# Spreading the reciprocals of the softmax sums over a tile: two products with the identity instead of a copy and a transpose

## The chip, the cores and the metric

One core of one Trainium2 chip. The metric is the device time of the whole kernel in microseconds (us). The engines: TensorE (PE, matrix products; PEld is its loading of the stationary operand), VectorE (DVE), ScalarE (ACT), GpSimd (POOL), SyncE (SP, which issues DMAs). Each engine executes its own instructions in order and waits for the others by semaphores.

## The reference

Three stages, each feeding the next, all fp32:

```python
# attention: q, k, v of 2 x 8 heads x 576 x 64
scores = q @ k.T / 8
kth = 32nd largest of each row
scores = where(scores >= kth, scores, -1e9)
attn = exp(scores - max); attn = attn / (sum(attn) + 1e-9)
x = (attn @ v), heads side by side          # 1152 x 512
# experts: 4 of 512 -> 1024 -> 512, weighted by the token's probabilities
x = sum over e of p[:, e] * (relu(x @ w1[e]) @ w2[e])
# last stage: 512 -> 768 three times, maximum, back to 512
out = max(x @ w1, x @ w2, x @ w3) @ w_out
```

## The kernel before

The 1152 tokens are nine tiles of 128, the 16 heads eight pairs of heads, four to a batch. A unit of the attention is one token tile of one head pair: 36 of them, called pairs here too, numbered `n` from 0. A pair computes the scores of both heads (`pss`, L475 or L483), finds the 32 largest of each row on VectorE (L513, L515), makes masked exponentials `p` with their row sums `rs` on ScalarE, turns `p` around with transposes on TensorE (`psp`, L559 and L564, copied to `pt` by ScalarE at L562 and L567), and multiplies with v.

The steps that the change touches come at the end of a pair. `guard` (L572, ACT) adds 1e-9 to the two sums of each token, and `recip` (L578, DVE) makes `rr`, 128 tokens x 2 heads, the reciprocals. The product with v stands transposed, `psv`, 128 features (64 of each head) x 128 tokens, so the reciprocals are needed as a tile of the same shape, the one of head j for token t in all rows j*64 to j*64+63 of column t. `spread` (L582, ACT) copies `rr` with a broadcast to `rb`, 128 tokens x 2 x 64. `trans_r` (L587, PE) transposes it to `psr`, and ACT copies that to `r` (L589). `norm` (L611, DVE) multiplies `psv` by `r`, which gives `xt`, and `split_x` (L624, ACT; L625, POOL) takes it apart into a high and a low half, `xh` and `xl`, for the expert stage's products.

`pv` (L591 to L606) is one product of 128 stationary columns (L601) and eight of 64 (L604): for each of four key tiles one for head 0, written to partitions 0 to 63 of `psv`, and one for head 1, written to partitions 64 to 127. An fp32 matmul shows as two records in the trace, a transpose as one.

The expert stage keeps its own products in flight beside the attention. A product of it is three matmuls of halves (L764, L765, L766); the halves of weights come from ACT (`whi`, L269) and from POOL or DVE (`wlo`, L275), the halves of the hidden layer from ACT and DVE, or, for every fourth hidden tile, from ACT (L902, L903) and POOL (L904). The first token tile uses whole fp32 weights (L850, L865).

The order is written by hand. A pair has eight slots, and tables of options (L39 to L45: FIRST, MIDDLE, TIGHT and so on, picked by `n`) say at which slot after `8 * n` a step stands; `at_slot` puts one step there, and `two` puts one there and its second half (the copy out of the bank) `lag` slots later. `rec` is the slot of the reciprocal, `pv` that of the product with v. Between slots the main loop places the expert stage's steps so that PE's budget of columns (`pe(...)`) keeps up with VectorE's (`dve(...)`). After the slots end, at about 446 us, the rest of the experts and the last stage run alone.

Of the kernel before, what the change touches and what calls it, by code (L numbers as in the profile page):

```python
# [10 lines left out]
F32 = mybir.dt.float32  # L11
# [3 lines left out]
AF = mybir.ActivationFunctionType  # L15
# [22 lines left out]

FIRST = dict(stag=2, new=1, scores=-12, trans=11, pv=17, rec=16, lag=2, sum=4, late=1)  # L39
MIDDLE = dict(stag=2, new=1, scores=-12, at=(11, 12), pv=14, rec=12, lag=1, sum=0, late=1)  # L40
TIGHT = dict(stag=3, new=1, scores=-7, at=(10, 11), guard=11, rec=11, spread=12, pv=12, turn=12, norm=13, split=13, last=14, lag=0, lag_s=1, sum=0, late=1)
SECOND = dict(TIGHT, norm=14, split=14, last=15)
THIRD = dict(stag=4, new=1, scores=-4, at=(11, 12), guard=12, rec=13, spread=13, pv=14, turn=14, norm=15, split=15, last=16, lag=0, lag_s=2, sum=0)
BOTH = dict(stag=4, new=1, scores=-4, at=(14, 14), pv=17, rec=15, lag=2, lag_t=1, sum=0, late=1)
LOOSE = dict(stag=4, new=1, scores=-4, at=(14, 14), pv=17, rec=15, split=22, last=24, lag=2, sum=0)  # L45

# [15 lines left out]
def kernel(  # L62
# [14 lines left out]
    nc = tc.nc  # L77
    B, HP, D, _, S = k.shape
    NT, DM = out.shape
    E = gates.shape[2]  # L80
    P = 128
# [13 lines left out]
    def batches(t):  # L95
        return (0, 1) if t == MIXED else (0 if t < MIXED else 1,)
# [16 lines left out]
    at = ctx.enter_context(tc.tile_pool(name="at", bufs=2))  # L113
# [7 lines left out]
    ident = const.tile([P, P], F32, name="ident")  # L121
# [12 lines left out]
    def pe(n):  # L134
        clock["pe"] += n / 2400.0

    def bank(name):
        return pg.tile([P, 512], F32, tag="g", name=name)
# [306 lines left out]
    class Pair:  # L445
# [131 lines left out]
            dve(60)  # L577
            nc.vector.reciprocal(out=self.rr, in_=self.rs)  # L578

        def spread(self):  # L580
            self.rb = at.tile([P, 2, D], F32, tag="rb", bufs=1, name="rb")
            nc.scalar.activation(out=self.rb, in_=self.rr.unsqueeze(2).to_broadcast([P, 2, D]), func=AF.Copy)  # L582

        def trans_r(self):
            ps = bank("psr")
            pe(260)
            nc.tensor.transpose(ps[:, 0:P], self.rb.rearrange("p a d -> p (a d)"), ident)  # L587
            self.r = at.tile([P, P], F32, tag="r", name="r")
            return lambda: [nc.scalar.activation(out=self.r, in_=ps[:, 0:P], func=AF.Copy), self.did.add("r")]  # L589

# [36 lines left out]
    def attention():  # L627

        NP = len(pairs)
        prs = {}  # L630
        later, between = {}, {}

        def options(n):
            return TIGHT if n == HP - 1 else SECOND if n == 2 * HP - 1 else MIDDLE if n in (HP - 2, 2 * HP - 3, 2 * HP - 2) else FIRST if n < 2 * HP else THIRD if n == 3 * HP - 1 else BOTH if n in ON_ACT[1] else LOOSE

        def at_slot(s, f, *a):
            later.setdefault(s, []).append((f, a))


        first_use = {}  # L640
        for n, (c, hp, t) in enumerate(pairs):
            for b in batches(t):
                if ("v", b, hp) not in first_use:
                    first_use["v", b, hp] = n
                    at_slot(8 * n + (options(n)["pv"] - 7 if b and hp else 0), load_v, b, hp)
                if t >= FULL:
                    first_use.setdefault(("k", b, hp), n)
            if t >= FULL and (t, hp) not in later_scores:
                first_use.setdefault(("q", c, hp), n)
            elif n and t < FULL:  # L650
                o = options(max(0, n - 2))
                at_slot(max(8 * n + options(n)["scores"] - LOAD_FULL, 8 * (n - 2) + o["scores"] + o["stag"] + 1), load_full, n)
        free = {"k": -99, "q": -99}
        for key, n in first_use.items():
            if key[0] == "v":
                continue
            s0 = 8 * n
            load, split = (load_k, split_k) if key[0] == "k" else (load_q, split_q)
            at = max(s0 + options(n)["scores"] - (SPLIT_K if key[0] == "k" else SPLIT_Q), free[key[0]] + 2)
            if key[0] == "k" and key[1] and key[2]:  # L660

                at = max(at, 8 * pairs.index((MIXED, key[2] - 1, MIXED)) + options(n)["scores"] + options(n)["stag"] + (1 if key[2] == HP - 1 else 4))
            at_slot(max(at - LOAD, free[key[0]] + 1), load, *key[1:])
            at_slot(at, split, *key[1:])
            free[key[0]] = at
        for n, (c, hp, t) in enumerate(pairs):
            s0 = 8 * n
            prs[n] = Pair(n)
            pr = prs[n]
            o = options(n)  # L670

            def two(s, f, *a, lag=o["lag"]):
                at_slot(s, lambda: at_slot(s + lag, f(*a)))
            for j in range(2):
                b0 = s0 + o["stag"] * j
                two(b0 + o["scores"] - SOONER * ((t, hp) in later_scores), pr.scores, j, lag=o.get("lag_s", o["lag"]))
                for i in range(7):
                    if o["new"]:
                        later.setdefault(b0 + i, []).insert(0, (pr.topk, (j, i)))
                    else:  # L680
                        at_slot(b0 + i, pr.topk, j, i)
                at_slot(b0 + 2, pr.negate, j)
                at_slot(b0 + 5, pr.exp, j)
                late = o.get("late", MASK_LATE) * pr.on_act[j]
                two(b0 + 7 + late, pr.mask, j, lag=o["sum"] if n < EARLY else 3)
                two(s0 + o["at"][j] if "at" in o else b0 + o["trans"] + late + (late > 0), pr.trans_p, j, lag=o.get("lag_t", o["lag"]))
            two(s0 + o["at"][1] if "at" in o else s0 + o["stag"] + o["trans"], pr.trans_p, 2, lag=o.get("lag_t", o["lag"]))
            at_slot(s0 + o.get("guard", o["rec"] - 1), pr.guard)
            at_slot(s0 + o["rec"], pr.recip)
            if o is LOOSE:  # L690
                at_slot(s0 + o["rec"], at_slot, s0 + o["rec"] + 1, pr.spread)
            else:
                at_slot(s0 + o.get("spread", o["rec"] + 1), pr.spread)
            at_slot(s0 + o["pv"], pr.pv)
            two(s0 + o.get("turn", o["rec"] + 2), pr.trans_r)
            end = max(o["pv"], o["rec"] + 2) + o["lag"]
            if n == 1:
                at_slot(s0, nc.sync.dma_start, gate, gates)
            if n == HP - 1:
                between.setdefault(s0 + o["norm"], []).append((norm_gates, ()))  # L700
            if "norm" in o:
                between.setdefault(s0 + o["norm"], []).append((pr.norm, ()))
            else:
                at_slot(s0 + end + 1, pr.norm)
            two(s0 + o.get("split", end + 2), pr.split_x)
        at_slot(-5, load_soon)
        two(9, two_soon, 0, lag=1)
        two(13, two_soon, 1, lag=3)
        for i, t in enumerate((7, *SOON_TWO, 6)):
            at_slot(17 + 3 * i, store_soon, t)  # L710
        last = {}
        for n, p in enumerate(pairs):
            o = options(n)
            last[p[0:2]] = 8 * n + o.get("last", max(o["pv"], o["rec"] + 2) + 2 * o["lag"] + 2)
        for n in range(len(alone)):
            at_slot(ALONE_FROM + ALONE_STEP * n, load_alone, n + 1)
        end = max(last.values()) + 1
        s = min(later)
        while s <= end:
            todo = later.pop(s, [])  # L720
            i = 0
            while i < len(todo):
                f, a = todo[i]
                f(*a)
                todo[i + 1:i + 1] = between.pop(s, [])
                todo += later.pop(s, [])
                i += 1
            if s > 8 * NP + 2:
                clock["dve"] += PAUSE
            yield s, [c for c in last if last[c] + (READY if c[1] == HP - 2 else 0) == s]  # L730
            s += 1

        while narrowed[0] < WIDE * len(wide):
            clock["dve"] += PAUSE
            yield s, []
            s += 1


    lag = []
# [31 lines left out]
    def begun(ps, wt, xs, N, parts):  # L771

        for f in range(2):
            for a in parts:

                product(spread(ps[:, f * N:(f + 1) * N], xs[0][a]), [w[:, a, f * P:(f + 1) * P] for w in wt], [x[a] for x in xs], f == a == 0, False)
            yield True
# [397 lines left out]
```

## Time and profile before

| | us |
|---|---|
| median of 3 runs | 735.45 (735.43 to 735.67) |
| the profiled execution, its own time | 734.86 |
| its span, first to last instruction | 733.0 |
| PE busy in the span | 715.2 (98%) |
| DVE, ACT, POOL busy | 580.2, 504.8, 476.7 |
| mean granted clock of TensorE | 1.00 |

The profiled execution is one run of the kernel under the hardware profiler; its span and the 1.86 us around it make its own time. Times of rows are from that one execution. The busy time of an engine is the union of its instructions. A PE record's duration includes its way through the array, so records overlap, and what one costs the next is read from start to start. An entry in square brackets says how long the engine stood still ahead of a row, and whose result ended that.

### The profile page before, as it was taken

How to read it: one execution, taken by the hardware profiler on the slowest of the kernel's cores; microseconds unless marked ns; L12 is line 12 of the kernel's file. 1: busy time of each engine (PE TensorE's matmuls, PEld its weight loads, DVE VectorE, ACT ScalarE, POOL GpSimd, SP SyncE). 2: the span in 40 equal slices, each digit the busy share in tenths (PEclk: the TensorE clock that was granted, in tenths of full speed). 3: DMA queues.
4: the chain of work that ended last, by engine and by line, in shares of the span. 5: the costliest groups of instructions: out<-in, count | busy, mean ns of one | idle time of the engine just before them, and what ended most of it. 6: DMA issues, size and time to landing. Idle time of an engine off the chain costs nothing. (4 is left out here: it accounts for less than half of the span.)

```text
span 733.0 us, 13786 instructions
## 1 busy us (share of the span) xinstructions
PE 715.2 (98%) x4758; PEld 637.1 (87%) x4758; DVE 580.2 (79%) x1174; ACT 504.8 (69%) x1127; POOL 476.7 (65%) x416
## 2 busy tenths in 40 slices
PE   5899999999999999999999999999999999999997
PEld 3687679889999998899988998999889998998996
DVE  7999989989999999999999974766879873323441
ACT  4868889899987886788888876556566753442431
POOL 2514779678989975879779867856745773532520
PEclk9999999999999999999999999999999999999999
DMA  8995555635756553555455436786879855543501
GB/s 238 303 281 203 146 180 156 181 113 165 208 154 197 150 164 111 170 170 177 137 165 173 139 122 216 267 299 209 294 238 338 256 189 211 167 147 114 188 1 43
DMA packets 57813, 135.26 MB, mean 185 GB/s; under 512 B 9936, under 2 KB 23120, under 8 KB 57744
## 3 DMA queue, kind: packets, MB, share of 16 engines
q1 hardware_dynamic: 49248, 125.74, 54.7%
q10 hardware_dynamic: 8496, 8.65, 3.4%
q8 instruction: 37, 0.61, 0.3%
q14 instruction: 32, 0.26, 0.1%
HBM read 123.36 MB, written 11.01 MB: 183 GB/s over the span
## 5 line engine op out<-in xcount | busy, mean ns | idle before, releaser
L275 POOL TENSOR_TENSOR wlo<-raw,whi 128x512 fp32r<-128x512 f32 x252 | 332.0, 1347 | 135.1 <-ACT whi L269 124.8
L269 ACT ACTIVATE whi<-raw 128x1024 fp32r<-128x1024 f32 x164 | 169.9, 1058 | 18.6 <-PE ps L766 10.2
L764 PE MATMUL ps<-xl,whi 128*128 128x256 f32 (+1 forms) x584 | 173.6, 297 | 0.5 <-POOL xl L625 0.5
L766 PE MATMUL ps<-xh,wlo 128*128 128x256 f32 (+1 forms) x584 | 170.7, 292 | 0.0
L765 PE MATMUL ps<-xh,whi 128*128 128x256 f32 (+1 forms) x584 | 170.6, 292 | 0.0
L513 DVE MAX8 m<-work 128x8 f32<-128x576 f32 x216 | 155.1, 744 | 0.1
L764 PEld LDWEIGHTS ps<-xl,whi 128*128 128x128 f32 x584 | 110.8, 190 | 1.6 <-POOL xl L625 0.7
L765 PEld LDWEIGHTS ps<-xh,whi 128*128 128x128 f32 x584 | 109.7, 188 | 0.9 <-issue 0.2
L766 PEld LDWEIGHTS ps<-xh,wlo 128*128 128x128 f32 x584 | 109.7, 188 | 0.0
L515 DVE MATCH_REPLACE8 work<-m,work 128x576 f32<-128x576 f32 x144 | 106.6, 741 | 0.0
L275 DVE TENSOR_TENSOR wlo<-raw,whi 128x1024 fp32r<-128x1024 f32 x38 | 54.7, 1445 | 49.7 <-ACT whi L269 36.8
L764 PE MATMUL ps<-wlo,h 128*128 128x512 f32 x224 | 91.0, 406 | 2.1 <-POOL wlo L275 1.9
L766 PE MATMUL ps<-whi,h 128*128 128x512 f32 x224 | 87.8, 392 | 0.0
L765 PE MATMUL ps<-whi,h 128*128 128x512 f32 x224 | 87.6, 391 | 0.0
L245 POOL TENSOR_TENSOR narrow<-narrow,raw 128x256 int32<-128x256 int32 x48 | 46.5, 976 | 21.3 <-DMA narrow<-narrow 5.7
L513 DVE MAX8 m<-s 128x8 f32<-128x576 f32 x71 | 53.1, 747 | 2.5 <-ACT s L495 2.5
L495 ACT ACTIVATE s<-pss 128x288 f32<-128x288 f32 x128 | 45.5, 401 | 12.0 <-PE pss L475 7.1
L515 DVE MATCH_REPLACE8 work<-m,s 128x576 f32<-128x576 f32 x72 | 53.3, 741 | 0.0
L764 PEld LDWEIGHTS ps<-wlo,h 128*128 128x128 f32 x224 | 42.8, 191 | 11.3 <-POOL wlo L275 5.0
L562 ACT ACTIVATE pt<-psp 128x512 f32<-128x512 f32 x72 | 40.0, 600 | 15.7 <-PE psp L559 15.6
L766 PEld LDWEIGHTS ps<-whi,h 128*128 128x128 f32 x224 | 42.1, 188 | 9.9 <-POOL h L904 0.5
L1042 DVE TENSOR_TENSOR tm<-ps,tm 128x384 f32<-128x384 f32 x36 | 19.8, 556 | 39.0 <-PE ps L766 39.0
(118 smaller groups left out, 1493.7 us busy)
## 6 DMA issues: line engine op xcount, KB each, us to landing
raw<-in_w_dram SPq DMA_DIRECT2D x128, 512.0 KB, 4.3
raw<-narrow SPq DMA_DIRECT2D x36, 512.0 KB, 4.5
raw<-in_m_dram SPq DMA_DIRECT2D x36, 256.0 KB, 5.1
whole<-in_w_dram SPq DMA_DIRECT2D x14, 512.0 KB, 5.5
narrow<-narrow ACTq DMA_DIRECT2D x48, 128.0 KB, 5.0
kraw<-in_k_dram SPq DMA_DIRECT2D x16, 288.0 KB, 4.5
raw<-in_mo_dram SPq DMA_DIRECT2D x12, 256.0 KB, 5.8
kfull<-in_k_dram SPq DMA_DIRECT2D x9, 288.0 KB, 5.2
```

What stands on the lines that cost most here:

```text
L245: nc.gpsimd.tensor_tensor(out=out.bitcast(I32), in0=out.bitcast(I32), in1=last, op=ALU.add)
L269: nc.scalar.activation(out=hi, in_=raw, func=AF.Copy)
L275: on.tensor_tensor(out=lo[:, x], in0=raw[:, x], in1=hi[:, x].bitcast(F32), op=ALU.subtract)
L495: nc.scalar.activation(out=s[:, h, :], in_=halves[h][:, 0:SH], func=AF.Copy)
L513: nc.vector.max(m[:, 8 * r:8 * r + 8], src)
L515: nc.vector.match_replace(out=self.w[j], in_to_replace=m[:, 8 * r:8 * r + 8], in_values=src, imm_value=NEG)
L562: return lambda: [nc.scalar.activation(out=d, in_=ps.rearrange("p (r n) -> p r n", r=NR), func=AF.Copy), self.did.add(("pt", part))]
L764: nc.tensor.matmul(ps, lhsT=lh, rhs=rl, start=first, stop=False)
L765: nc.tensor.matmul(ps, lhsT=lh, rhs=rh, start=False, stop=False)
L766: nc.tensor.matmul(ps, lhsT=ll, rhs=rh, start=False, stop=last)
L1042: nc.vector.tensor_tensor(out=tm[:, g], in0=ps, in1=tm[:, g], op=ALU.max)
```

## The change

The copy `spread` goes, with its places in the option tables. `trans_r` becomes two matmuls into the same bank: for each head j the stationary operand is column j of `rr`, read 64 times with stride zero, and the moving operand is the identity; the result, 64 partitions x 128 tokens, goes to partitions j*64 to j*64+63 of `psr`. `trans_r` now stands at the slot of `pv`. The copy to `r` and all that follows stay. The budget entry of `trans_r`, `pe(260)`, stays.

```diff
--- before.py
+++ after.py
@@ -38,9 +38,9 @@
 
 FIRST = dict(stag=2, new=1, scores=-12, trans=11, pv=17, rec=16, lag=2, sum=4, late=1)
 MIDDLE = dict(stag=2, new=1, scores=-12, at=(11, 12), pv=14, rec=12, lag=1, sum=0, late=1)
-TIGHT = dict(stag=3, new=1, scores=-7, at=(10, 11), guard=11, rec=11, spread=12, pv=12, turn=12, norm=13, split=13, last=14, lag=0, lag_s=1, sum=0, late=1)
+TIGHT = dict(stag=3, new=1, scores=-7, at=(10, 11), guard=11, rec=11, pv=12, norm=13, split=13, last=14, lag=0, lag_s=1, sum=0, late=1)
 SECOND = dict(TIGHT, norm=14, split=14, last=15)
-THIRD = dict(stag=4, new=1, scores=-4, at=(11, 12), guard=12, rec=13, spread=13, pv=14, turn=14, norm=15, split=15, last=16, lag=0, lag_s=2, sum=0)
+THIRD = dict(stag=4, new=1, scores=-4, at=(11, 12), guard=12, rec=13, pv=14, norm=15, split=15, last=16, lag=0, lag_s=2, sum=0)
 BOTH = dict(stag=4, new=1, scores=-4, at=(14, 14), pv=17, rec=15, lag=2, lag_t=1, sum=0, late=1)
 LOOSE = dict(stag=4, new=1, scores=-4, at=(14, 14), pv=17, rec=15, split=22, last=24, lag=2, sum=0)
 
@@ -577,14 +577,11 @@
             dve(60)
             nc.vector.reciprocal(out=self.rr, in_=self.rs)
 
-        def spread(self):
-            self.rb = at.tile([P, 2, D], F32, tag="rb", bufs=1, name="rb")
-            nc.scalar.activation(out=self.rb, in_=self.rr.unsqueeze(2).to_broadcast([P, 2, D]), func=AF.Copy)
-
         def trans_r(self):
             ps = bank("psr")
             pe(260)
-            nc.tensor.transpose(ps[:, 0:P], self.rb.rearrange("p a d -> p (a d)"), ident)
+            for j in range(2):
+                nc.tensor.matmul(ps[j * D:(j + 1) * D, 0:P], lhsT=self.rr[:, j:j + 1].to_broadcast([P, D]), rhs=ident, start=True, stop=True)
             self.r = at.tile([P, P], F32, tag="r", name="r")
             return lambda: [nc.scalar.activation(out=self.r, in_=ps[:, 0:P], func=AF.Copy), self.did.add("r")]
 
@@ -687,12 +684,8 @@
             two(s0 + o["at"][1] if "at" in o else s0 + o["stag"] + o["trans"], pr.trans_p, 2, lag=o.get("lag_t", o["lag"]))
             at_slot(s0 + o.get("guard", o["rec"] - 1), pr.guard)
             at_slot(s0 + o["rec"], pr.recip)
-            if o is LOOSE:
-                at_slot(s0 + o["rec"], at_slot, s0 + o["rec"] + 1, pr.spread)
-            else:
-                at_slot(s0 + o.get("spread", o["rec"] + 1), pr.spread)
             at_slot(s0 + o["pv"], pr.pv)
-            two(s0 + o.get("turn", o["rec"] + 2), pr.trans_r)
+            two(s0 + o["pv"], pr.trans_r)
             end = max(o["pv"], o["rec"] + 2) + o["lag"]
             if n == 1:
                 at_slot(s0, nc.sync.dma_start, gate, gates)
```

VectorE, GpSimd and SyncE keep their orders. TensorE's changes in place only in pairs 0 and 4. Here is TensorE around the product with v in pair 4, before (`psp` are the transposes of the next pair's exponentials, `pss` scores, `hfull` and `whole` the first tile's expert products):

```order
L564 MATMUL psp<-ident,p 128x128
L865 MATMUL ps_783<-whole,hfull 128x512 x4
L601 MATMUL psv<-pt_807,v_last_112 128x128
L604 MATMUL psv<-pt,vt 64x128 x8
L475 MATMUL pss<-kfull,qfull 128x288 x2
L587 MATMUL psr<-ident,rb 128x128
L559 MATMUL psp<-ident,p 128x128 x4
L865 MATMUL ps_783<-whole,hfull 128x512
```

and the same place after the change, where lines have smaller numbers:

```order
L564 MATMUL psp<-ident,p 128x128
L858 MATMUL ps_779<-whole,hfull 128x512 x4
L598 MATMUL psv<-pt_803,v_last_112 128x128
L601 MATMUL psv<-pt,vt 64x128 x8
L584 MATMUL psr<-ident,rr 64x128 x2
L475 MATMUL pss<-kfull,qfull 128x288 x2
L559 MATMUL psp<-ident,p 128x128 x4
L858 MATMUL ps_779<-whole,hfull 128x512
```

The two products for `psr` stand ahead of the two score products, where the transpose stood behind them. In the other pairs but 0 the place is the same. TensorE in pair 22, whose transpose starts at about 284 us, before:

```order
L766 MATMUL ps_3978<-xh,wlo 128x256
L601 MATMUL psv<-pt_3958,v_last_113 128x128
L604 MATMUL psv<-pt,vt 64x128 x8
L587 MATMUL psr<-ident,rb 128x128
L764 MATMUL ps_4045<-xl,whi 128x256
L765 MATMUL ps_4045<-xh,whi 128x256
```

and after:

```order
L759 MATMUL ps_3954<-xh,wlo 128x256
L598 MATMUL psv<-pt_3936,v_last_113 128x128
L601 MATMUL psv<-pt,vt 64x128 x8
L584 MATMUL psr<-ident,rr 64x128 x2
L757 MATMUL ps_4022<-xl,whi 128x256
L758 MATMUL ps_4022<-xh,whi 128x256
```

Two products of 64 stationary columns stand in the place of one transpose. ScalarE in the same pair, before (`rs` are the sums, `raw` and `h` the hidden tile that POOL takes, `whi` a weight's high half):

```order
L572 ACTIVATE rs<-rs 128x2
L520 ACTIVATE nb<-m_3929 128x1
L562 ACTIVATE pt<-psp 128x512 x2
L567 ACTIVATE pt_3958<-psp 128x128
L582 ACTIVATE rb<-rr 128x128
L902 ACTIVATE raw<-ps_3767 128x512
L903 ACTIVATE h<-raw 128x512
L269 ACTIVATE whi<-raw 128x1024 x2
```

and after:

```order
L572 ACTIVATE rs<-rs 128x2
L520 ACTIVATE nb<-m_3907 128x1
L562 ACTIVATE pt<-psp 128x512 x2
L567 ACTIVATE pt_3936<-psp 128x128
L895 ACTIVATE raw<-ps_3746 128x512
L896 ACTIVATE h<-raw 128x512
L269 ACTIVATE whi<-raw 128x1024 x2
```

The copy to `rb` is gone, and the reading of the hidden tile's bank follows the last copy to `pt`.

## Rows read from the trace of the kernel before

**Rows 1.** The page's first part: busy us (share of span) and instructions, by engine.

```profile
PE 715.2 (98%) x4758; PEld 637.1 (87%) x4758; DVE 580.2 (79%) x1174; ACT 504.8 (69%) x1127; POOL 476.7 (65%) x416
```

**Rows 2.** Windows: stretch, its us; busy PE, PEld, DVE, ACT, POOL; clock, DMA, GB/s.

```profile
30.00:60.00 30.00, 29.60 (x231) 24.64 (x232) 29.86 (x71) 23.26 (x70) 5.04 (x7) 1.00 0.95 285
60.00:160.00 100.00, 96.93 (x668) 78.53 (x667) 92.17 (x201) 88.71 (x221) 72.47 (x67) 1.00 0.50 151
160.00:446.00 286.00, 285.11 (x2202) 257.59 (x2201) 270.87 (x576) 232.42 (x543) 237.29 (x204) 1.00 0.54 163
```

**Rows 3.** Groups by line (busy us, mean ns | idle before); L587 in 160:446 (min/median/max).

```profile
L587 PE MATMUL psr<-ident,rb 128*128 128x128 f32 x36 | 11.8, 328 | 0.1
L582 ACT ACTIVATE rb<-rr 128x128 f32<-128x128 f32 x36 | 11.5, 318 | 7.4 <-DVE rr L578 7.3
L587 PE MATMUL psr<-ident,rb x24: 327/328/330, 164.4 to 444.8; 128*128 128x128 f32 x24
```

**Rows 4.** Timeline of PE, 443.7 to 445.5 us: start, us, instruction; second row: last pair.

```profile
443.75 1.09 PE L604 MATMUL psv<-pt,vt 128*64 128x128 f32 x16
444.57 0.28 PE L604 MATMUL psv<-pt,vt 128*64 128x128 f32 x2
444.78 0.33 PE L587 MATMUL psr<-ident,rb 128*128 128x128 f32 x1
444.86 0.48 PE L764 MATMUL ps<-wlo,h 128*128 128x512 f32 x1
445.18 0.39 PE L765 MATMUL ps<-whi,h 128*128 128x512 f32 x1
445.41 0.40 PE L766 MATMUL ps<-whi,h 128*128 128x512 f32 x1
```

**Rows 5.** Timeline of PE, eight transposes of exponentials.

```profile
439.70 1.04 PE L559 MATMUL psp<-ident,p 128*128 128x128 f32 x8
```

**Rows 6.** Timeline of PE behind score products in 64-row tiles, 73.8 us.

```profile
73.80 0.70 PE L865 MATMUL ps<-whole,hfull 128*128 128x512 f32 x1
...
74.33 0.59 PE L865 MATMUL ps<-whole,hfull 128*128 128x512 f32 x1
```

**Rows 7.** Timeline of ACT, 280.7 to 283.5 us.

```profile
280.75 0.29 ACT L567 ACTIVATE pt<-psp 128x128 f32<-128x128 f32 x1
282.68 0.31 ACT L582 ACTIVATE rb<-rr 128x128 f32<-128x128 f32 x1 [1.64 <-DVE rr L578]
282.89 0.58 ACT L902 ACTIVATE raw<-ps 128x512 f32<-128x512 f32 x1
```

**Rows 8.** Timeline of POOL, 284 to 291 us.

```profile
284.21 1.30 POOL L904 TENSOR_TENSOR h<-raw,h 128x512 fp32r<-128x512 f32 x1 [4.26 <-ACT h L903]
285.47 5.58 POOL L275 TENSOR_TENSOR wlo<-raw,whi 128x512 fp32r<-128x512 f32 x4
```

**Rows 9.** Timeline of PE, 289 to 291.6 us; three products between these two.

```profile
288.98 0.40 PE L766 MATMUL ps<-whi,h 128*128 128x512 f32 x1
...
291.10 0.50 PE L764 MATMUL ps<-wlo,h 128*128 128x512 f32 x1 [0.78 <-POOL wlo L275]
```

**Rows 10.** Waits of weight loads, 160:446 (us in total, times, longest).

```profile
PEld psp L564 <- ACT s L495: 0.6, 2, 0.3
PEld psv L601 <- ACT pt L567: 0.5, 2, 0.3
```

**Rows 11.** Waits of PE, 60:160.

```profile
PE ps L764 <- POOL wlo L275: 1.1, 4, 0.3
PE psv L601 <- ACT pt L567: 1.0, 2, 0.7
```

**Rows 12.** Timeline of DVE around pair 11's reciprocal.

```profile
144.52 0.15 DVE L578 RECIPROCAL rr<-rs 128x2 f32<-128x2 f32 x1
144.59 1.40 DVE L513 MAX8 m<-work 128x8 f32<-128x576 f32 x2
```

**Rows 13.** Timeline of PE, pair 11's transpose.

```profile
145.45 0.33 PE L587 MATMUL psr<-ident,rb 128*128 128x128 f32 x1
```

## The prediction

> **What bounds the kernel now.** First the page's line of busy times: TensorE (PE) is busy for 715 of the 733.0 us of the span [rows 1]. Then the windows by stage: what an edit is worth depends on whether PE or something that feeds it is late there. In 30 to 60 us VectorE (DVE) is busy for 29.86 of 30 us, in 60 to 160 us no engine is full (PE idle for 3.07 of 100 us, DVE at 92%, ScalarE (ACT) at 89%), and in 160 to 446 us PE is busy for 285.1 of 286 us [rows 2]. The granted clock of TensorE is 1.00 (its 2.4 GHz level) in each of them, so no term here is one of the clock. Third, the groups by line and shape: where the edited instructions lie. There are 36 transposes at L587 and 36 copies at L582 that feed them; 24 of the transposes start between 164.4 and 444.8 us, in the stretch in which PE decides, and none later [rows 3]. Last, PE's timeline around one transpose, because a matmul's duration (328 ns) is not what it holds PE for: starts count.
>
> **PE, per pair.** Removed: one transpose. Added: two products of 64 stationary columns each, written to the two halves of the partitions. That is the shape of the eight products at L604 that stand directly ahead, and it is the way the order shows them in 34 of 36 pairs. Around 444.8 us the sixteen records of L604 (two for each fp32 product) start within 443.75 to 444.57 in eight pairs, seven steps in .82 us or .12 each; the two of a pair run together [rows 4]. Eight transposes at L559 take 1.04 us, of which the last lasts some .28 like the last pair of L604: (1.04 - .28)/7 = .109 from one to the next [rows 5]. I take .109 for a pair of small records too, the first of L604's steps being longer by what precedes it. The transpose at L587 starts .21 after the last pair, the next product .08 after the transpose, and the one after that .32 later, where such products follow each other by .23 [rows 4]. So the transpose costs about .08 + .09 = .17 us; the .20 ahead of it is the way from 64-column to 128-column tiles and is paid by whatever comes next. After the change: four records in two pairs, 2 x .109 = .218, then the .20, then the next product. One thing comes on top: the first 128-wide product after small tiles takes about .11 longer than its like (.70 against .59 us, L865 at 73.80 and 74.33 [rows 6]). I take +.10. Sum: .218 + .10 - .17 = **+.15 us per pair**. The bounds: if nothing is exposed behind the small tiles, .218 - .17 = +.05; if the two halves do not run together, 4 x .109 - .17 + .10 = +.37. I take the value between, because L604, directly ahead and of the same tiles, pairs up. The stationary operand of stride zero has no row of its own; I cost its load as that of L604's.
>
> In 160 to 446 us this is 24 x .15 = **+3.6 us** on the engine that decides. Nothing covers it: PE is idle there for .9 us in all.
>
> **ACT.** Removed: 36 copies of 318 ns, 11.5 us, and the 7.4 us for which ACT stood still ahead of them, nearly all for the reciprocal of DVE [rows 3]. ACT executes in order, so whatever is queued behind such a copy waits with it. At 282.68 us this can be followed to PE: ACT is through at 281.04, waits 1.64 us for the reciprocal, copies, and only then reads L902's bank (.21 after the copy's start) [rows 7]. From there L903 gives POOL the tile for which it has waited 4.26 us, POOL makes one h and four wlo until 291.05 [rows 8], and PE, which goes through four steps between 288.98 and 291.10 that take .23 each elsewhere, needs 2.12 us for .92: a stall of 1.2 us, plus .1 in the longer first product behind it [rows 9]. Without the copy this chain may begin up to 1.85 us sooner (1.64 + .21), more than the 1.3 us of the stall: **-1.3 us**. What is late next there is PE itself. Weight loads that waited in this stretch for other results of ACT, psp for s (.6) and psv for pt (.5), are 1.1 us in four places [rows 10]; most of these wait for chains that begin at a PE event and have no such copy in them. I take **-0.2**, a fifth; the bounds are 0 and -1.1.
>
> **Before 160 us.** Twelve pairs. Up to 60 us DVE is full [rows 2], its order and work do not change, and PE's extra time lies beside it. In 60 to 160 us PE waits for wlo (1.1 us) and for pt (1.0 us) [rows 11]: chains of POOL and ACT set the pace, and PE's extra .15 falls into such waits. If nothing is covered, 12 x .15 = +1.8. If ACT sets the whole pace in the eight pairs of this stretch, each copy gives back the .21 for which it holds its follower [rows 7]: -1.6. I take **+0.1**, as the two nearly cancel.
>
> **What moves.** DVE, POOL and SP keep their orders. On PE only pairs 0 and 4 have the new products ahead of score products that stood ahead of the transpose; on ACT the copy of psr goes ahead of a few instructions in the same two pairs, both before 160 us and within the bounds above. No DMA is moved. The new products wait for DVE's reciprocal directly, no longer through ACT. The tightest pair: the reciprocal ends at 144.67, and its place on PE is just ahead of 145.45, some .7 us later [rows 12, 13]. So I cost this wait at nothing; its cover is that .7 us. Behind the products PE queues everything, and ACT's copy r and DVE's norm follow at the old distance, with .15 more.
>
> **Sum.** +0.1 + 3.6 - 1.3 - 0.2 = +2.2 us. The profiled execution took 734.86 us, its span 733.0, and the 1.86 us around it stay: 737.1. The median of the runs is .59 above the profiled one, so 735.45 becomes **737.6**. With the ends of the costs: 24 x .05 gives 735.3; +1.8 before 160 us and no -0.2 give 739.6.
>
> **Rivals.**
> *More relief (B).* ACT's 19 us also carried the other short waits: all 1.1 us of [rows 10] go, and the pairs before 160 us give .2 back. +3.6 - 1.3 - 1.1 - 0.2 = +1.0: 736.5, no change to be told. For it: ACT is the engine that ended most of these waits. Against it: most of those chains hold no such copy.
>
> *Faster (C).* The transpose holds PE for its whole record, 328 ns [rows 3], not .17. Then the exchange is .218 + .10 - .33 = -.01 per pair, 24 of them -0.2, and the gains on ACT are left: +0.1 - 0.2 - 1.3 - 0.2 = -1.6, so 733.9. It decides from a hold of .32 upwards. Against it: the next product starts .08 after the transpose [rows 4], and transposes at L559 follow each other by .109 [rows 5]. The Trainium skill ("TensorE: Matmul & The Clock Gate", Part 4, on PE-mode transpose) gives about 275 ns for a 128x128 transpose within a kernel; as an estimate from that page the exchange would be +.04 per pair. The rows do not agree with that as a hold of PE: .11 from start to start is what they show.
>
> *Much slower (D).* The two halves follow each other instead of running together, or the load of stride zero is slow by as much: +.37 in 24 pairs is +8.9; 8.9 + 0.1 - 1.3 - 0.2 = +7.5: 743. Against it: sixteen records of L604 in .82 us [rows 4], in the same tiles. The Trainium skill (same page, Part 3, what overlaps) says that a weight load overlaps matmuls in flight only where the row group differs; the two halves here differ in columns alone, so by that rule they would not. The starts of L604 speak against that rule as a cost of .11 for each record.
>
> *It does not do what it says (E).* The wait for ACT becomes one for DVE on PE itself, which holds all products. If one more VectorE operation of .7 us, like the two behind the reciprocal at 144.59 (1.40 for both) [rows 12], were to stand ahead of it in relation to PE, the cover would be just gone; with two, a pair loses .7. In four pairs as tight as that one, +2.8 on top of +2.2: 740.4. The reciprocal's place on DVE does not change and PE gets later, not sooner, so I give it little.
>
> **How the numbers follow.** About 0.2%, 1.47 us, is what a measurement of this kernel can tell from no change. Forecast .56 (.03 of it within that bound), B .25, C .10, D .07, E .02. Faster: C, .10. Same: .25 + .03 = .28. Slower: .53 + .07 + .02 = .62. The range reaches over the forecast's own ends and B and leaves out C, D and E (.19): 735.4 to 739.6.
>
> **What would show it.** In PE's timeline psr as four records in two pairs .11 apart, right behind the sixteen of L604, the next product .20 later and its follower .1 later than its like: then +.15 holds. Starts of psr's records .11 apart one by one would be D. No 128x128 copy from rr on ACT, L902's place reached up to 1.85 us sooner against its neighbours, and no wait for wlo at the place of 291 us: then -1.3 holds; if a wait for wlo stays there, the stall had another cause, and the time is up to 739. The point at which the last psr ends should lie 2.2 us later than 445.1, and the rest should take what it took. The waits of PE in 60 to 160 us should shrink by about what the products add. What would make it wrong most easily is the cost per pair: .05 more or less of it is 1.2 us.

## The result and the profile after

The changed kernel takes 740.48 us (median of 6 runs) against 735.56 us of the kernel before, measured together. One of the six runs took 4023 us; why is not known, and the ratio is that of the others. They have a median of 740.32 us and, by their means, a ratio of 1.0059 with a 95% interval of 1.0042 to 1.0075, or 3.1 to 5.5 us more. The direction was forecast; the size, 737.6 with a range up to 739.6, was too small.

The profiled execution has a span of 738.4 us, 5.4 more than before. The page's busy times:

```profile
PE 720.7 (98%) x4866; PEld 643.3 (87%) x4866; DVE 580.2 (79%) x1174; ACT 497.7 (67%) x1091; POOL 476.3 (65%) x416
```

Against [rows 1]: PE has 108 records more (36 pairs, four records for one) and 5.5 us more of busy time, ACT 36 instructions and 7.1 us less (less than the 11.5 us of the copies, whose records overlap with their followers), DVE and POOL are as before. The timeline of PE around the last of the 36 places, which answers to [rows 4] (start, us, instruction):

```profile
448.48 0.61 PE L601 MATMUL psv<-pt,vt 128*64 128x128 f32 x8
448.91 0.39 PE L584 MATMUL psr<-ident,rr 128*64 128x128 f32 x4
449.23 0.50 PE L757 MATMUL ps<-wlo,h 128*128 128x512 f32 x1
449.57 0.40 PE L758 MATMUL ps<-whi,h 128*128 128x512 f32 x1
449.80 0.39 PE L759 MATMUL ps<-whi,h 128*128 128x512 f32 x1
```

The four records of psr last .39 together and, by the next row, .273 each, so the last starts .12 after the first. In the trace they start at 448.913, 448.919, 449.022 and 449.029: two pairs, .109 apart, the two records of a pair together. Whether such two are of the two halves of the partitions, or the two records of one product, the trace does not tell; the price does not depend on it. From their start to the next product it is .32, and from that to its follower .34. In [rows 4] the last pair of L604, at 444.57, is followed by the product after next at 445.18, .61 later. Here the last pair of L601 (448.48 + .61 - .28 = 448.81) is followed by it at 449.57, .76 later. So a pair of the attention costs PE +.15 us, as the prediction had it.

The groups by line that answer to [rows 3] (busy us, mean ns | idle before) are these, the last one the weight load of the new products:

```profile
L584 PE MATMUL psr<-ident,rr 128*64 128x128 f32 x144 | 14.0, 273 | 0.0
L586 ACT ACTIVATE r<-psr 128x128 f32<-128x128 f32 x36 | 9.8, 273 | 14.3 <-PE psr L584 14.3
L584 PEld LDWEIGHTS psr<-ident,rr 128*64 128x64 f32 x144 | 8.9, 137 | 0.0
```

The weight loads of L604 in the kernel before, as its line's instructions are listed (ns: least, median, most; starts; forms):

```profile
L604 PEld LDWEIGHTS psv<-pt,vt x640: 132/137/138, 26.9 to 444.5; 128*64 128x64 f32 x160
```

The load with stride zero takes 137 ns, the median of the ordinary load of 64 columns in the kernel before. Of the 7.4 us for which ACT stood still ahead of the copy, 3.3 came back at the reading of psr (11.0 before, 14.3 now).

**Where the time went.** PE's products come in the same order in both kernels, but for the edited ones. So the start of a product can be compared with that of the same product before, and the difference followed through the span. Positive is later than before, in us; each column is one product, named by its start in the kernel before.

| kernel | 69.16 | 159.98 | 288.52 | 291.10 | 317.54 | 318.28 | 444.86 | 612.53 | 638.57 |
|---|---|---|---|---|---|---|---|---|---|
| changed kernel | +.11 | +.36 | +2.16 | +.95 | +1.22 | +2.79 | +4.37 | +4.39 | +5.34 |

Read between the columns: the stretch of the 24 pairs, from 160 to 446 us, gives 1.80 + .27 + 1.58 = 3.65, or .15 each. Followed across each of the 24 places alone, from the last product ahead of psr to the fourth behind it, the sum is 3.74, with a median of .16. The stall at 291 us gave back 1.21. **A new stall of 1.57 us** stands at 318 us, which the prediction did not have. After 446 us there is nothing, except .95 at 618 us. The waits of PE in the changed kernel of 160 to 450 us are one row (us in total, times, longest us), where the stall of [rows 9] stood before:

```profile
PE psp L564 <- DVE h L904: 1.6, 1, 1.6
```

The waits of weight loads in [rows 10] are still there, and went from 1.1 to .7 us:

```profile
PEld psv L598 <- ACT pt L567: 0.4, 2, 0.2
PEld psp L564 <- ACT s L495: 0.3, 1, 0.3
```

Here is the place of the new stall in the changed kernel's timeline of PE, and the end of that wait in its timeline of VectorE:

```profile
318.33 1.03 PE L559 MATMUL psp<-ident,p 128*128 128x128 f32 x8
320.99 0.33 PE L564 MATMUL psp<-ident,p 128*128 128x128 f32 x1 [1.62 <-DVE h L904]
321.07 0.36 PE L757 MATMUL ps<-xl,whi 128*128 128x256 f32 x1
```

```profile
318.94 1.40 DVE L513 MAX8 m<-work 128x8 f32<-128x576 f32 x2
320.26 0.67 DVE L904 SCALAR_TENSOR_TENSOR h<-ps,h 128x512 fp32r<-128x512 f32 x1
```

In the kernel before, the same transpose follows the eight ahead of it without a wait:

```profile
317.11 1.04 PE L559 MATMUL psp<-ident,p 128*128 128x128 f32 x8
318.20 0.33 PE L564 MATMUL psp<-ident,p 128*128 128x128 f32 x1
318.28 0.36 PE L764 MATMUL ps<-xl,whi 128*128 128x256 f32 x1
```

L564 transposes exponentials. It has no use for h; what it waits for is its bank of PSUM. VectorE reads a hidden tile out of it at 320.26, behind two operations of its own. In the kernel before, the same transpose got a bank of scores, which ScalarE had read by then, and the hidden tile stood in another. The two programs say how widely that holds: of the 508 tiles that PE fills in PSUM, 418 lie in another bank than their counterpart, the tile of the same name and the same turn. The kernel asks a pool of six banks for 449 of them and does not say which (391 of these moved), and a pool of two for the rest. The edit was enough to turn the hand-out around; which part of it did so, no run separates.

### The profile page after: what moved, and what is told of

The parts are those of the page before. It is cut to its first block, busy times and chain, and to the rows that moved or that the text cites. A ratio compares the mean times of both kernels' runs of the same rounds, so it can differ in the third digit from the quotient of the medians.

```text
span 738.4 us, 13982 instructions
## 1 busy us (share of the span) xinstructions
PE 720.7 (98%) x4866; PEld 643.3 (87%) x4866; DVE 580.2 (79%) x1174; ACT 497.7 (67%) x1091; POOL 476.3 (65%) x416
## 4 chain that ended last, share of the span: by engine, by line
PE 82%; DVE 5%; DMA 3%; ACT 3%; issue 3%; POOL 3%; SPq 1%; ACTq 0%; POOLq 0%; DVEq 0%
PE ps L757 20%; PE ps L759 19%; PE ps L758 19%; PE psv L601 4%; PE psp L559 4%; PE pss L483 3%; DVE m L513 2%; PE pso L757 2%; PE psa L843 2%; PE pso L758 2%; PE pso L759 2%; POOL wlo L275 1%; PE psv L598 1%; PE ps L858 1%; PE pss L475 1%
## 5 line engine op out<-in xcount | busy, mean ns | idle before, releaser
L757 PEld LDWEIGHTS ps<-wlo,h 128*128 128x128 f32 x224 | 42.1, 188 | 11.5 <-POOL wlo L275 3.6
```

Of the source, the lines that this page charges most:

```text
L757: nc.tensor.matmul(ps, lhsT=lh, rhs=rl, start=first, stop=False)
```

## The experiments

Each runs against the kernel before on the same chip. Medians move by chance with the first 50 us, where PE waits for the first loads: two profiles of the same program, the changed one, reach the product at 69 us .11 and 1.76 us later than before. So terms are read from the profiles, between columns as above; the medians give the whole, and the intervals of the ratios below reach 1.2 to 2.1 us to either side. Three kernels (PE late, products in pair 22 alone, products made twice) ran on another chip than the other seven.

### Banks, place and products apart

All kernels of the experiments keep a table that says for each of the tiles which of the six banks it gets. This is the edit, cut at the dots; the digits are those of the kernel whose banks are wanted, and one more call of the pool, in the last stage, is changed in the same way:

```diff
-    pg = ctx.enter_context(tc.tile_pool(name="pg", bufs=6, space=PSUM))
+    pgs = [ctx.enter_context(tc.tile_pool(name="pg%d" % i, bufs=1, space=PSUM)) for i in range(6)]
+    PINS = list("0543210543210543210524310432104532104521452312315231253125304120435120431520..." )
     def bank(name):
-        return pg.tile([P, 512], F32, tag="g", name=name)
+        return pgs[int(PINS.pop(0))].tile([P, 512], F32, tag="g", name=name)
```

**The products, old place, old banks.** Beside the table, `two(s0 + (o["rec"] + 2 if o is FIRST else o["pv"]), pr.trans_r)`, which puts the products of pairs 0 and 4 where the transpose stood.

> The two products of the change, at the place where the transpose stood, and every PSUM tile of the six shared banks put by a table into the bank that its counterpart has in the kernel before. Theory 1 (the bank decides): the wait of 1.62 us on TensorE for VectorE's h ahead of the transpose L564 at 321 us, which the kernel before does not have, is there because that tile was given the bank of a hidden tile. Here the wait is gone, and the time is 1.5 us below the changed kernel, about 738.8 to 739.0 us (735.56 + 4.92 - 1.5). Theory 2 (the products or the missing copy shift the engines against each other, and the wait comes from that): the wait stays, and the time is that of the changed kernel, 740.5 us. By both, the wait of 1.2 us for wlo at 291 us stays away.

Measured: 738.54 us, ratio 1.0027 (1.0004 to 1.0049). No wait at 318 us.

**Copy and transpose, new place, new banks.**

> The copy on ScalarE and the one transpose of the kernel before, but at the place of the changed kernel (the slot of the product with v), and every PSUM tile in the bank that it has in the changed kernel. Theory 1 (the bank decides): a wait for VectorE's h of 1 to 2 us ahead of L564 near 320 us, with copy and transpose as before; the wait for wlo at 291 us stays too, since the copy is there; 735.56 + 1.5 = 737.0 us. Theory 2: no wait near 320 us, 735.6 us.

Its edit, beside the table, is in the kernel before: `two(s0 + o["pv"], pr.trans_r)` in place of `two(s0 + o.get("turn", o["rec"] + 2), pr.trans_r)`.

Measured: 737.56 us, ratio 1.0021 (1.0004 to 1.0037). The wait near 320 us is there, with copy and transpose as before.

These two change place and banks together. Two more change the banks alone:

> The changed kernel in its own order, only that every PSUM tile of the six shared banks is put into the bank that its counterpart has in the kernel before. If the banks alone make the wait of 1.6 us at 321 us: no wait there, about 738.5 us like the run with the old place as well. If the new place in the pairs 0 and 4 has a part in it, or the products: up to 740.5 us.

Measured: 738.46 us, ratio 1.0030 (1.0008 to 1.0052). This kernel's timeline of PE at the place of the wait:

```profile
318.12 1.03 PE L566 MATMUL psp<-ident,p 128*128 128x128 f32 x8
319.18 0.33 PE L571 MATMUL psp<-ident,p 128*128 128x128 f32 x1
319.27 0.36 PE L764 MATMUL ps<-xl,whi 128*128 128x256 f32 x1
```

> The kernel before, copies, transposes and order as there, with the banks of the changed kernel. If the banks alone make the wait: one of 1.5 to 2 us ahead of L564 near 320 us, and 735.6 + 1.6 = 737.2 us. The 0.8 to 1.0 us that the run with copy, transpose, new place and new banks lost ahead of 50 us should not be there, if they come from the new place of a transpose that still waits for ScalarE's copy; if they are there, they come from the banks too, and the time is 738.0 us.

Measured: 737.41 us, ratio 1.0023 (1.0006 to 1.0041). The instructions are those of the kernel before, to the last one, and this is its timeline of PE:

```profile
317.82 1.04 PE L566 MATMUL psp<-ident,p 128*128 128x128 f32 x8
320.68 0.33 PE L571 MATMUL psp<-ident,p 128*128 128x128 f32 x1 [1.82 <-DVE h L918]
320.76 0.36 PE L771 MATMUL ps<-xl,whi 128*128 128x256 f32 x1
```

And a second run of the changed kernel, with its own banks written out:

> The changed kernel again, its banks written out in the table and the same as there: the time of the changed kernel, 740.5 us, and the wait of 1.6 us at 321 us. The wait of 1.2 us for wlo at 624 us, which ends with the landing of a DMA, should differ from that of the first profile if it is chance.

Measured: 740.88 us, ratio 1.0062 (1.0041 to 1.0083). It starts 1.65 us later than the first profile and keeps that; the wait at 318 us is the same, and the wait at 618 us did not go: 1.1 us of PE's there. The starts of the same products, as in the table above:

| kernel | 69.16 | 159.98 | 288.52 | 291.10 | 317.54 | 318.28 | 444.86 | 612.53 | 638.57 |
|---|---|---|---|---|---|---|---|---|---|
| changed, again | +1.76 | +2.09 | +3.81 | +2.60 | +2.88 | +4.42 | +6.00 | +6.02 | +6.90 |
| products, old place and banks | +.11 | +.48 | +2.16 | +.95 | +1.22 | +1.19 | +2.78 | +2.80 | +2.64 |
| products, new place, old banks | -.10 | +.15 | +1.94 | +.74 | +1.01 | +.99 | +2.61 | +2.63 | +3.58 |
| copy, new place, new banks | +.81 | +.97 | +.98 | +.98 | +1.04 | +2.81 | +2.60 | +2.60 | +2.55 |
| copy, old place, new banks | +.54 | +.58 | +.66 | +.65 | +.72 | +2.48 | +2.28 | +2.28 | +2.26 |

Between 317.54 and 318.28 stand 1.54 to 1.77 in the rows with the new banks and nothing in those with the old ones, whatever the instructions and their place. The pool of two banks, which the table leaves alone, is no rival: its tiles lie as in the changed kernel in all five of these rows, with the wait and without it. By the medians, new banks cost 737.41 - 735.67 = 1.7 us with the copy and 740.88 - 738.46 = 2.4 us with the products; the products cost 738.46 - 735.67 = 2.8 us with the old banks and 3.5 with the new ones. The theory of the banks holds, and that the products or the missing copy bring the wait about is out. The .8 to 1.0 us that the copy at its new place lost before 69 us is within what the two profiles of the changed kernel differ by, so it says nothing on the place.

The wait at 618 us ends with the landing of a DMA (raw from narrow, for which ACT waits and then DVE's wlo and PE). PE waits .2 us there in the kernel before, and 1.0 to 1.2 us in four profiles: the changed kernel, its second profile, the products with old banks at the new place and the next experiment. These are the ones with the products at the new place, but for the kernel with the products made twice, which comes 13 us late and waits .3 us. The products with old banks at the old place, which differ from those at the new place neither in PE's work nor in the median, do not have it either. That the second profile repeats it speaks against mere chance. The changed kernel's page has the chain in its waits from 604 to 630 us:

```profile
PEld pso L757 <- DVE wlo L275: 1.6, 1, 1.6
DVE wlo L275 <- ACT whi L269: 1.6, 1, 1.6
ACT whi L269 <- DMA raw<-narrow: 1.5, 1, 1.5
```

What makes that DMA land later in some profiles stays open. The medians of the two kernels with products and old banks, 738.46 and 738.54 us, do not show the wait that one of their profiles has and the other has not.

### The copy on ScalarE

The changed kernel with the copy kept, unread:

```diff
+        def spread(self):
+            self.rb = at.tile([P, 2, D], F32, tag="rb", bufs=1, name="rb")
+            nc.scalar.activation(out=self.rb, in_=self.rr.unsqueeze(2).to_broadcast([P, 2, D]), func=AF.Copy)
...
+            at_slot(s0 + o.get("spread", o["rec"] + 1), pr.spread)
```

> The changed kernel, banks as there, with the copy of the reciprocals to 128x128 on ScalarE kept at its old place; nobody reads it. If the copy's wait for the reciprocal made the stall of 1.2 us at 291 us, that stall comes back, and the time is about 1.2 us above the changed kernel: 741.7 us. If the stall went away for another reason (the products, the banks, another state of the queue on GpSimd), the time is that of the changed kernel, 740.5 us, and TensorE does not wait for wlo there.

Measured: 740.60 us, ratio 1.0064 (1.0043 to 1.0084), the time of the changed kernel. The stall at 291 us is gone with the copy in place (288.52: +2.91, 291.10: +1.70, a gain of 1.21). So its removal was not needed for that. The next run makes PE late without touching anything else:

```diff
-            nc.tensor.transpose(ps[:, 0:P], self.rb.rearrange("p a d -> p (a d)"), ident)
+            for _ in range(3 if 16 <= self.n <= 21 else 1):
+                nc.tensor.transpose(ps[:, 0:P], self.rb.rearrange("p a d -> p (a d)"), ident)
```

> The kernel before, banks as there, ScalarE's copies and the transposes kept, with two more transposes into the same place in each of the pairs 16 to 21 (207 to 275 us): 12 x .109 = 1.3 us more on TensorE ahead of the stall at 291 us, and nothing else. Theory A (the copy's wait for the reciprocal makes the stall, and only its removal takes it away): the stall stays at 1.2 us, the time is 735.6 + 1.3 = 736.9 us. Theory B (the stall is a chain through ScalarE and GpSimd that VectorE's reciprocal times, and a later TensorE comes to it with less to wait): the stall shrinks to 0.3 us or less, the time is 735.6 to 735.9 us.

Measured: 736.93 us, ratio 1.0028 (1.0005 to 1.0050), by the median as theory A has it. The profile says otherwise: the profiled execution took 735.60 us; .54 us of its lateness come from before 69 us, 1.40 are added by 288.52, and behind the stall the product at 291.10 is +.75, that at 444.86 +.60.

| kernel | 69.16 | 159.98 | 288.52 | 291.10 | 317.54 | 318.28 | 444.86 | 612.53 | 638.57 |
|---|---|---|---|---|---|---|---|---|---|
| PE late by 12 transposes | +.54 | +.54 | +1.94 | +.75 | +.62 | +.63 | +.60 | +.60 | +.77 |
| products in pair 22 alone | +1.99 | +2.01 | +2.20 | +1.01 | +1.34 | +1.34 | +1.34 | +1.34 | +1.41 |

The stall took in 1.2 of the 1.4 us. The median is of runs that scatter by more than the term (735.48 to 743.06 us), so I go by the profile: theory B. A late start alone does not use the stall up: in the two rows with the copy and new banks all engines are .7 and 1.0 us late together, and the product at 291.10 is as late as that at 288.52. And the copy alone, in the pair ahead of the stall (its copy to `rb` is left out too):

```diff
+            if self.n == 22:
+                for j in range(2):
+                    nc.tensor.matmul(ps[j * D:(j + 1) * D, 0:P], lhsT=self.rr[:, j:j + 1].to_broadcast([P, D]), rhs=ident, start=True, stop=True)
+            else:
                 nc.tensor.transpose(ps[:, 0:P], self.rb.rearrange("p a d -> p (a d)"), ident)
```

> The kernel before, banks as there, with the two products in the place of copy and transpose in one pair alone, number 22, whose copy stands ahead of the chain that ends in the stall at 291 us. TensorE is not late here but for .16 us. Theory A (the copy holds the chain): GpSimd's h starts up to 1.85 us sooner than 284.21 us, the stall of 1.2 to 1.3 us is gone, and the time is 735.6 - 1.2 + .16, about 734.5 us. Theory B alone (only TensorE's being late takes the stall away): the stall stays, 735.6 us.

Measured: 735.18 us, ratio .9989 (.9971 to 1.0007), not to be told from the kernel before. In the profile the stall is gone here too: from +2.20 to +1.01. Of that, .33 is lost again by 317.54, where PE now comes sooner to a wait for VectorE. ACT's timeline in this kernel, where the hidden bank is read right behind the last copy to pt, and POOL's, where h starts sooner:

```profile
282.80 0.29 ACT L574 ACTIVATE pt<-psp 128x128 f32<-128x128 f32 x1
282.95 0.62 ACT L915 ACTIVATE raw<-ps 128x512 f32<-128x512 f32 x1
```

```profile
284.31 1.29 POOL L917 TENSOR_TENSOR h<-raw,h 128x512 fp32r<-128x512 f32 x1 [2.32 <-ACT h L916]
```

At 280 us of this kernel PE, DVE, ACT and POOL are all 2.0 us later than before, as they are from 60 us on; against that, h at 284.31 is 1.9 us sooner than the 284.21 of [rows 8] would make it. **Both theories hold, and either alone is enough**: the copy held the chain that ends in the stall by 1.9 us, and a PE that comes 1.3 us later finds the same stall used up. In the changed kernel both act on one stall, which can be taken away once. There, ACT's timeline shows a wait for PE, 1.52 us, in the place of that for the reciprocal, since PE's transposes are late by then; POOL's h is below it:

```profile
281.90 1.09 ACT L562 ACTIVATE pt<-psp 128x512 f32<-128x512 f32 x2 [1.52 <-PE psp L559]
282.88 0.28 ACT L567 ACTIVATE pt<-psp 128x128 f32<-128x128 f32 x1
283.03 0.62 ACT L895 ACTIVATE raw<-ps 128x512 f32<-128x512 f32 x1
```

```profile
284.39 1.30 POOL L897 TENSOR_TENSOR h<-raw,h 128x512 fp32r<-128x512 f32 x1 [3.66 <-ACT h L896]
```

POOL's h starts at 284.39, .18 later than in [rows 8], while PE is 2.16 late. Of the 1.85 us by which the prediction let the chain start sooner, nothing is seen in the clock; it is seen only against PE.

### The price of a pair

```diff
-            for j in range(2):
+            for j in (0, 1, 0, 1):
                 nc.tensor.matmul(ps[j * D:(j + 1) * D, 0:P], lhsT=self.rr[:, j:j + 1].to_broadcast([P, D]), rhs=ident, start=True, stop=True)
```

> The changed kernel, banks as there, with every pair's two products made twice into the same place (four fp32 products, eight records). If the two halves run together, the second pair of products takes two steps of .109: +.218 for each pair, 24 x .218 = 5.2 us from 160 to 446 us on the engine that decides there, and up to 12 x .218 = 2.6 us before, most of it covered: 740.5 + 5.2 to 7.8, about 746 to 748 us, less what the remaining stalls absorb (1.6 at 321 us, which hangs on VectorE and not on TensorE): 744.5 to 748. If the halves follow each other, .436 for each pair: 10.5 us more, 751 us or above.

Measured: 747.20 us, ratio 1.0155 (1.0139 to 1.0171). From 318.28 to 444.86 its lateness grows from +9.00 to +13.30, 4.30 us, where the changed kernel's grows by 1.58. These are the last eleven pairs, so the added pair of products costs 2.72 in all, .25 each; the sum for two steps of .109 is .218, that for four steps .436. Across the places alone, lateness grows by .37 at the median of 24 pairs, .22 more than in the changed kernel, and the rest of the .25 lies elsewhere. So two products take two steps and not four. The wait at 318 us is nearly used up here (8.78 to 9.00), since PE comes 9 us late to it.

### The reciprocal written wide

The kernel before, with the reciprocal itself making the 128x128 tile on VectorE and no copy:

```diff
-            nc.vector.reciprocal(out=self.rr, in_=self.rs)
+            nc.vector.reciprocal(out=self.rb, in_=self.rs.unsqueeze(2).to_broadcast([P, 2, D]))
```

> The kernel before, banks as there, but with the reciprocal itself writing the 128x128 tile on VectorE from the sums read with stride zero; ScalarE's copy is gone, the transpose stays. TensorE's work is that of the kernel before. If the terms found so far hold: -1.2 us for the stall at 291 us, which hung on the copy, and 36 times about 0.12 us more on VectorE (a 128x128 operation takes 0.27 us there, the reciprocal of 128x2 0.15), of which only the pairs before 60 us, where VectorE is full, count in full: +0.4. So 734.8 us. If the stall at 291 us does not hang on the copy: 736.0 us.

Measured: 749.81 us, ratio 1.0183 (1.0155 to 1.0211). The expectation took .27 us, the price of a multiplication of that size. A reciprocal of 128x128 takes .94, as its group by line in this kernel has it:

```profile
L585 DVE RECIPROCAL rb<-rs 128x128 f32<-128x128 f32 x36 | 33.8, 938 | 0.6 <-ACT rs L579 0.5
```

36 x (.94 - .15) = 28 us more on VectorE; half of it reached the end, also in the stretch in which PE decides: by 444.86 the products are 13.06 late, from 6.09 at 160 us. The run says what VectorE costs when it becomes late. On the copy it says little: at 291 us the stall is gone here too, with PE 7.9 us late.

## Why the prediction was wrong

- **PE, per pair: right.** +.15 forecast, .15 to .16 seen in 24 pairs (3.65 to 3.74 us for 3.6). The working holds in its parts: two steps of .11, .21 to the next product, .34 to its follower. The load of stride zero costs what L604's costs.
- **ACT, the stall at 291 us: right in size, short in cause.** -1.3 forecast, -1.21 seen. The copy did hold that chain (products in pair 22 alone). But the products' own lateness would have used up the stall with the copy in place (copy kept, PE late), so the two edits do not add: the step "the copy goes, so the stall goes" should have asked first how late PE comes there. By the prediction's own sum it comes 11 x .15 = 1.65 us late.
- **Before 160 us: in its bounds.** +.1 forecast; +.36 at 159.98 in the profile, in a stretch whose start moves by 1.6 us between two profiles of one program. PE's waits in 60 to 160 us shrank from 2.9 to 2.2 us, as forecast in kind.
- **The -.2 of other waits: .1 at most.** The places of the 24 pairs add up to 3.74 and their stretch to 3.65, so .09 came back outside them.
- **What moves: the step that failed.** It went through the order on five engines and found two pairs of 36 changed, "within the bounds above". The order on the engines was read rightly. Left out was what the order also decides: which bank each tile gets, and so which reader it waits for. 418 of 508 tiles moved, one of them behind a late VectorE operation, at +1.6 us in the stretch in which PE decides. So "within the bounds above" put at nothing a term that was half of the miss. With the old banks the changed kernel takes 738.46 us, within the range; the new ones put it above.
- **The rest "should take what it took": it did not.** The last psr ends 4.2 us later than before, not 2.2, and the wait for a DMA at 618 us adds .95; what causes that wait is open. In the profile the forecast was +2.2 and the product at 638.57 is +5.34: the banks make 1.57 of the 3.1 between them, this wait .95, the start before 160 us .26, and the rest, .36, is mostly what the stall at 291 us and the other waits gave less than forecast.
- **The rivals.** Faster (C), a transpose that holds PE for its whole record, is out: .15 for a pair, not -.01. Much slower (D) is out: products made twice cost .22 to .25 more for a pair, not .44. The rule that was named for D, by which a weight load overlaps matmuls in flight only where the row group differs, stands in the Trainium skill ("TensorE: Matmul & The Clock Gate", Part 3, what overlaps). It is on weight loads, and the trace does not agree with it: the last two loads of psr (137 ns each, from 448.914 and 448.921) run while the products that start at 448.913 and 448.919 (273 ns each, on the same 128 rows) are in flight. More relief (B) did not come. E, a wait for the reciprocal on PE, did not come either: the row of waits from 160 to 450 us has the banks' wait alone. That E's price, 740.4 us, is near the measured time is chance.
- **What would have warned.** Of the two programs, the waits of each instruction can be laid side by side; the transpose at 318 us waits for ScalarE in one and for VectorE in the other, and that needs no chip. The prediction named what to look for at psr, at 291 us and at the end, but no row for a wait at a place that the change does not touch.

## What to carry to other kernels

Where tiles come from a pool without a name, any edit that removes or moves a user may turn the hand-out around: compare the banks and the waits of the whole program, not just the order near the edit, and fix the banks by a table when two variants are to be compared. A stall on the deciding engine is a store of time that can be spent once, on less work in the chain that makes it or on more work on the engine that waits. And a cost on the engine that decides (.15 us, 24 times) goes to the end but for the one stall that it finds, while 19 us of freed and idle time on another gave at most that stall.

## What the runs showed that was not expected

- VectorE's reciprocal grows with the tile: .15 us for 128x2, .94 us for 128x128, where a multiplication of two 128x128 tiles takes .27.
- A stationary operand read with stride zero costs no more to load than an ordinary one (137 ns for 64 columns in both).
- The first 50 us, with all loads under way, move by up to 2 us between executions of this kernel (+.11 and +1.76 at the same product for one program, +1.99 in another kernel that does the same work until then). The intervals from about a dozen runs reach 1.2 to 1.7 us to either side; the starts of the same products, in two profiles of one program, differ by 1.65 us at 69 us and by that within .1 from there to the end.
